# Reordering the head of a fused state-space and gated-MLP kernel: which engine copies tiles 0 and 1, when tile 2 and tile 3 are normalised, and where tile 2 and tile 3 are transposed

## The chip, the cores and the metric

The kernel runs on one core of a Trainium2 chip. The metric is the device time of one execution in microseconds (us), the median of several runs. A profile of one execution, taken by the hardware profiler, gives every instruction of the five engines: TensorE (PE, its weight loads are shown as PEld), VectorE (DVE), ScalarE (ACT), GpSimd (POOL) and SyncE (SP, which issues most DMAs).

## The reference

The input x has 2048 tokens of 448 features. Each row is normalised, xn = (x - mean) / sqrt(var + 1e-5). Two branches read xn:

```
Bu = xn @ B_bar^T ; h[t] = Lam_bar * h[t-1] + Bu[t] (complex, 448 states)
s  = 2 * Re(h @ C^T) + xn * Dskip
m  = (sigmoid(xn @ w_gate) * (xn @ w_up)) @ w_down     (448 -> 1792 -> 448)
out = x + s * silu(m)
```

## The kernel before, in words

The 2048 tokens are worked in four chunks of 512, each of four tiles of 128 tokens. TensorE contracts over partitions, so it needs xn with the features on the partitions: every tile is transposed. For chunks 1 to 3 a DMA does that. For chunk 0, at the head of the kernel, where everything waits for the first tiles, TensorE transposes each normalised tile against an identity matrix into PSUM and ScalarE or VectorE copies the result to SBUF (`xnT`).

The path of a tile of chunk 0 is: statistics (`bn` and `aggr` on VectorE, lines 431 to 439; for tile 2 `act_mean` and `act_var` on ScalarE, lines 471 to 477), square root on ScalarE (`root`, `act_root`, lines 466 and 479), reciprocal and normalisation on VectorE (`recip`, `norm`, lines 462 and 514), transposition on TensorE (`pe_transpose`, line 542, for tile 0; `row_transpose`, line 561, for tiles 1 to 3), and the copy (`pe_transpose` itself for tile 0, one half by VectorE and one by ScalarE; `pair_copy`, line 554, for tile 1; `row_copy`, line 572, for tiles 2 and 3: tile 2's halves go to ScalarE and VectorE, tile 3's both to VectorE).

The 448 features are held as 7 blocks of 64 rows. The products use half of the array's rows at a time: two products run side by side, one on the lower 64 rows (LO) and one on the upper 64 (UP), each 64 rows deep. A step of the gate product (one m of seven, 256 of the 1792 columns) has two PSUM banks, and each bank takes seven such products. `z_mm` (line 783) issues the pair with one product for each bank; `ph_mm(u, 0)` (line 791) issues three pairs in which LO writes bank 0 and UP bank 1; `ph_mm(u, 1)` issues three pairs the other way round. When a bank is to be written by the other half of the rows than before, `row_mm` makes the product wait until the other half's last product there is done:

```
774   pe_n[0] += 1
775   other = None if start else wrote.get((bank, 1 - h))
...
778   if other and other[0] > seen[0]:
779       tc.add_manual_dep(T.nop().ins, other[1].ins.name, SYNC, reason="other rows' product in this bank")
```

The nop's wait is put on the weight load or product behind it.

The first three gate steps of chunk 0 cannot wait for all four tiles, so they are cut (lines 1111 and 1112): `units[t]` holds tile t's 128 tokens of steps 0 and 1 (banks gu0 and gu1), `pairs[0]` and `pairs[1]` the tokens of tiles 0 and 1, and of 2 and 3, of step 2 (gu2, 256 tokens). `front` (line 1120) of a list issues `ph_mm(u, 0)` and `z_mm(u)` of each unit, `back` (line 1125) issues `ph_mm(u, 1)`. Before the change TensorE's order is: tile 0's transposition; `columns` (line 602), five small products that turn three parameter rows into columns, in the bank of tile 0's second half; `fill(5)`, five products that nothing uses; tile 1's transposition, into gu2; front and back of unit 0; front of unit 1; tile 2's transposition, into the two `acc` banks; back of unit 1; front of pair 0; front of unit 2; tile 3's transposition; back of unit 2; back of pair 0; front of unit 3; front of pair 1; back of unit 3; back of pair 1. Gate step 3 follows in the `acc` banks (`one(0, 3, "g", ...)`, line 1173), and then all other work of chunk 0. The results of steps 0 to 2 leave PSUM through ScalarE (`gu_evac`, line 843, Tanh at line 853).

The order on the engines comes from a planner inside the kernel (`Plan`). Each operation is added with an engine, a cost, the keys it reads and writes, and for the head (`pl.seq = True`) TensorE, VectorE and ScalarE keep the order in which operations are added. Behind the head (line 1172 on) VectorE and ScalarE choose by due times that the planner works out, so a change of the head can move their later operations. SyncE and the DMA issues keep their order. `gate` adds a point without an instruction, which orders keys. `silu_table` (line 636) loads the second activation table on ScalarE once all square roots are done, `turns` and `scale` start the rotation tables on GpSimd and ScalarE.

Of the kernel before, what the change touches and what calls it, by code (L numbers as in the profile page):

```python
# [14 lines left out]
ACT = mybir.ActivationFunctionType  # L15
# [6 lines left out]
P = 128  # L22
# [52 lines left out]
class Plan:  # L75
# [10 lines left out]
    def add(self, eng, cost, fn, r=(), w=(), dma=0, lat=None, chain=False, name="", rate=230e3):  # L86
        o = Op()
        o.idx, o.eng, o.cost, o.fn, o.dma, o.name = len(self.ops), eng, cost, fn, dma, name
        o.lat = LAT.get(eng, 0.0) if lat is None else lat
        o.pre, o.suc, o.rate = {}, [], rate  # L90
        o.slot, o.land = None, 0.0
        if dma and eng != "POOL":
            o.slot, self.n_dma = self.n_dma, self.n_dma + 1
        o.start = o.end = None
        for k in r:
            if k in self.w:
                self._edge(self.w[k], o, True)
        for k in w:
            for q in self.r.get(k, ()):
                self._edge(q, o, False)  # L100
            if k in self.w:
                self._edge(self.w[k], o, True)
        for k in w:
            self.w[k] = o
            self.r[k] = []
        for k in r:
            if k not in w:
                self.r.setdefault(k, []).append(o)
        if chain or eng == "PE" or (eng in ("DVE", "ACT") and self.seq):
            key = ("chain", eng)  # L110
            if key in self.last_of:
                self._edge(self.last_of[key], o, None)
            self.last_of[key] = o
        self.ops.append(o)
        return o
# [132 lines left out]
def kernel(  # L248
# [213 lines left out]
    def recip(t0, n):  # L462
        ks = lambda k: [(k, t) for t in range(t0, t0 + n)]
        add("DVE", 0.08, lambda: V.reciprocal(out=rsd[:, t0:t0 + n, :], in_=sdb[:, t0:t0 + n, :]), r=ks("sd"), w=ks("rs"))

    def root(t, n=1):
        ts = range(t, t + n)
        add("ACT", 0.2, lambda: A.activation(sdb[:, t:t + n, :], mvf[:, t:t + n, 1:2], ACT.Sqrt, bias=epsc[:]),
            r=[("mv", q) for q in ts] + ["sqrttab", "epsc"], w=[("sd", q) for q in ts], lat=0.16)
# [5 lines left out]
    def act_var(t):  # L475
        add("ACT", 0.7, lambda: A.activation(junk[:], x_all[:, t, :], ACT.Square, bias=nmf[:, t, :], accum_out=sqf[:, t, :]),
            r=[("x", t), ("nf", t)], w=[("mv", t), "junk"])
# [36 lines left out]
    def norm(t, eng="DVE"):  # L514
        b, o, x = xkey(t), pieces(xbuf(t), 256, 256), pieces(x_all[:, t, :], 192, 256)
        if t < TPC:
            s1, op0 = (nmf[:, 2, :], ALU.add) if t == 2 else (mvf[:, t, 0:1], ALU.subtract)
            e, cost = (V, 0.36) if eng == "DVE" else (G, 0.7)
            add(eng, cost, lambda: e.tensor_scalar(out=o, in0=x, scalar1=s1, scalar2=rsd[:, t, :], op0=op0, op1=ALU.mult),  # L519
                r=[("x", t), ("mv", t), ("rs", t)], w=[("xn", b)])  # L520
        else:
            r = [("x", t), ("rs", t), ("nm", t)]
            if t < 2 * TPC:
                add("DVE", 0.36, lambda: V.tensor_scalar(out=o, in0=x, scalar1=rsd[:, t, :], scalar2=nmr[:, t, :],
                                                         op0=ALU.mult, op1=ALU.add), r=r, w=[("xn", b)])
            else:
                add("ACT", 0.7, lambda: A.activation(o, x, ACT.Identity, bias=nmr[:, t, :], scale=rsd[:, t, :]), r=r, w=[("xn", b)])
# [14 lines left out]
    def pe_transpose(t, keys, banks):  # L542
        o, js = xbuf(t), slice(t * P, t * P + P)
        for i, (key, bank) in enumerate(zip(keys, banks)):
            tp = flat(bank.bitcast(BF16)[:, 0:2 * P], 2, P)

            def f(i=i, tp=tp):
                for s in range(2):
                    T.transpose(tp[:, s, :], o[:, (2 * i + s) * P:(2 * i + s + 1) * P], ident[:, :])  # L549
            add("PE", 0.15, f, r=[("xn", xkey(t)), "ident"], w=[key])  # L550
            eng, cost, e = (("DVE", 0.28, V.tensor_copy), ("ACT", 0.33, A.copy))[i]
            add(eng, cost, lambda e=e, i=i, tp=tp: e(out=xnT[0][:, 2 * i:2 * i + 2, js], in_=tp), r=[key], w=[("xnT", 0, t, i)])

    def pair_copy(t, a, eng):
        js = slice(t * P, t * P + P)
        src = gu[a][:].bitcast(BF16)[:, :, 0:4 * H].rearrange("p h (s j) -> p s h j", j=H)
        e, cost = (A.copy, 0.57) if eng == "ACT" else (V.tensor_copy, 0.45)
        add(eng, cost, lambda: e(out=xnT[0][:, :, js].rearrange("p s (h j) -> p s h j", j=H), in_=src),
            r=[("gu", a, 0), ("gu", a, 1)], w=[("xnT", 0, t, 0), ("xnT", 0, t, 1)])

    def row_transpose(t, keys, banks):
        o = xbuf(t)
        tp = [flat(bank.bitcast(BF16)[:, 0:4 * H], 4, H) for bank in banks]

        def f():
            for s in range(4):
                for h, (hs, _, _) in enumerate((LO, UP)):
                    T.transpose(tp[h][:, s, :], o[hs, s * P:s * P + P], ident[hs, hs])
        add("PE", 0.13, f, r=[("xn", xkey(t)), "ident"], w=keys)
        return tp  # L570

    def row_copy(t, h, key, tp):
        js = slice(t * P + h * H, t * P + h * H + H)
        eng, cost, e = (("ACT", 0.33, A.copy), ("DVE", 0.25, V.tensor_copy))[h or t == 3]
        add(eng, cost, lambda: e(out=xnT[0][:, :, js], in_=tp), r=[key], w=[("xnT", 0, t, h)])
# [60 lines left out]
    def silu_table():  # L636
        add("ACT", 1.3, lambda: A.preload_act_table_set("silu_and_others"), r=[("sd", t) for t in range(4)] + [("xnT", 0, 2, 0), "pv0"], w=["silutab"])
# [153 lines left out]
    def ph_mm(u, i, qs=(0, 1, 2), start=False, stop=False):  # L791
        out, w, x, r, keys, banks, n, name = u

        def f():
            for q in qs:
                for h, (hs, ss, _) in enumerate((LO, UP)):
                    b = 1 - h if i else h
                    row_mm(banks[b], h, lambda: T.matmul(out[b], lhsT=w(b, hs, ss[q]), rhs=x(b, hs, ss[q]),  # L798
                                                         start=start and q == 0, stop=stop and q == 2), start and q == 0)
        add("PE", len(qs) * (0.0028 + n / 2400.0), f, r=r, w=keys, name=name)  # L800
# [295 lines left out]
    u2 = slots0[2]  # L1096
# [6 lines left out]
    aggr(1)  # L1103
    norm(0)
    root(1)
    act_var(2)
    recip(1, 1)
    norm(1)
    uk, ub = [("gu", u2, 0), ("gu", u2, 1)], [gu[u2][:, 0, :], gu[u2][:, 1, :]]
    ak, ab = [("acc", 0), ("acc", 1)], [acc[0][:], acc[1][:]]  # L1110
    units = [[gu_unit(0, "g", m, slots0[m], t, t + 1) for m in range(2)] for t in range(TPC)]
    pairs = [gu_unit(0, "g", 2, u2, t, t + 2) for t in (0, 2)]

    def fill(n):
        def f():
            for _ in range(n):
                T.matmul(gu[slots0[0]][:, 0, 0:P], lhsT=ones[:, 0:P], rhs=ones[:, 0:P], start=True, stop=True)  # L1117
        add("PE", 0.055 * n, f, w=[("gu", slots0[0])])

    def front(us, start=False):  # L1120
        for u in us:
            ph_mm(u, 0, start=start)
            z_mm(u, False)

    def back(us, stop=False):
        for u in us:
            ph_mm(u, 1, stop=stop)

    pe_transpose(0, ak, ab)
    copy_pv = columns(acc[1][:, 400:412], "pvps")  # L1130
    fill(5)
    act_root(2)
    row_transpose(1, uk, ub)
    pair_copy(1, u2, "ACT")
    bn(3)
    recip(2, 1)
    norm(2)
    aggr(3)
    copy_pv()
    add("NONE", 0.0, lambda: None, r=["pv0", ("xn", 0)], w=["pv"], lat=0.0)  # L1140
    front(units[0], True)
    back(units[0])
    front(units[1])
    root(3)
    tp = row_transpose(2, ak, ab)
    for h in range(2):
        row_copy(2, h, ak[h], tp[h])
    recip(3, 1)
    norm(3)
    silu_table()  # L1150
    back(units[1])
    gate(uk, ("gu", u2))
    front(pairs[0:1], True)
    front(units[2])
    tp = row_transpose(3, ak, ab)
    for h in range(2):
        row_copy(3, h, ak[h], tp[h])
    back(units[2])
    back(pairs[0:1])
    turns()  # L1160
    scale(0)
    front(units[3])
    front(pairs[1:])
    back(units[3], True)
    back(pairs[1:], True)
    gu_evac(0, "g", 0, slots0[0])
    gu_evac(0, "g", 1, slots0[1])
    gu_evac(0, "g", 2, slots0[2])
# [113 lines left out]
```

## Time and profile before

| | us |
|---|---|
| median of 3 runs (lowest, highest) | 182.67 (182.58, 182.85) |
| the profiled execution's own time | 182.58 |
| its span, first to last instruction | 180.8 |
| around the span | 1.78 |
| DVE busy | 162.3 (90%) |
| ACT busy | 107.2 (59%) |
| POOL busy | 26.4 (15%) |
| tile 0's transposition starts on PE | 5.32 |
| gate step 3 starts on PE | 11.59 |

The span begins with the first instruction and ends with the last; the time has what lies around it as well. A matmul's row has its start and a modelled end; products are pipelined, so the next one starts before the row of the one before ends. A line of the timeline merges rows of one kind that follow each other: start, length, engine, line of the kernel, operation, what it writes and reads, shape and count. In brackets stands how long the engine was idle ahead of it and what ended that.

### The profile page before, as it was taken

The numbers are of one execution on the slowest core, as the hardware profiler recorded it, in microseconds if no ns is written. First come the engines' busy times: TensorE is split into PE (matmuls) and PEld (weight loads), VectorE is DVE, ScalarE is ACT, GpSimd is POOL, SyncE is SP. The second block draws the span as 40 slices with busy tenths as digits, with TensorE's granted clock in tenths as the row PEclk, the third lists the DMA queues.
The fourth block names the chain that finished last, engine by engine and source line by source line (L and its number), as shares of the span: only waits on it lengthen the run. The fifth ranks groups of instructions, "written<-read, shape, count | busy, mean of one in ns | idle before, by whom it ended". The sixth has DMA issues, their size and how long they took to land.

```text
span 180.8 us, 3804 instructions
## 1 busy us (share of the span) xinstructions
PE 176.8 (98%) x1507; PEld 89.5 (49%) x1507; DVE 162.3 (90%) x300; ACT 107.2 (59%) x175; POOL 26.4 (15%) x76
## 2 busy tenths in 40 slices
PE   8999999999999999999999999999999999999993
PEld 2775555564544444445554444454554444455552
DVE  2776899999997889999999998999999999999572
ACT  3889992966698898473265333599221599711100
POOL 5374224000028118600000000000000000000000
DMA  5999833998000320000032000000000000012131
GB/s 151 370 362 243 127 60 63 300 235 231 1 0 0 62 58 0 4 0 0 4 62 56 0 4 0 0 29 25 25 2 4 0 0 0 4 51 75 54 119 39
DMA packets 23941, 12.73 MB, mean 70 GB/s; under 512 B 14833, under 2 KB 23922, under 8 KB 23922
## 3 DMA queue, kind: packets, MB, share of 16 engines
q1 hardware_dynamic: 23568, 12.24, 26.9%
q8 instruction: 12, 0.20, 0.5%
q10 hardware_dynamic: 290, 0.23, 0.4%
q14 instruction: 7, 0.06, 0.1%
q0 software_dynamic: 64, 0.00, 0.0%
HBM read 7.23 MB, written 1.84 MB: 50 GB/s over the span
## 4 chain that ended last, share of the span: by engine, by line
PE 95%; DMA 2%; DVE 1%; SPq 0%; issue 0%; DVEq 0%
PE gu L798 42%; PE gu L1015 15%; PE acc L1034 10%; PE acc L1015 9%; PE acc L798 9%; PE gu L788 7%; DMA x_all<-in_A_x_dram 2%; PE gu L1034 1%; PE acc L788 1%; DVE o_t L1076 0%; DVE bst L433 0%; DVE o_t L1070 0%; PE acc L549 0%; SPq L360 0%; PE gu L1117 0%; DVE g_t L519 0%
## 5 line engine op out<-in xcount | busy, mean ns | idle before, releaser
L798 PE MATMUL gu<-xnT,wU 64*128 64x512 bf16 x288 | 41.8, 376 | 0.0
L798 PE MATMUL gu<-xnT,wG 64*128 64x512 bf16 (+2 forms) x348 | 37.9, 325 | 0.0
L1015 PEld LDWEIGHTS <-hF 128*128 128x128 bf16 x224 | 21.7, 98 | 21.2 <-issue 1.3
L1015 PE MATMUL gu<-wd,hF 128*128 128x448 bf16 x140 | 28.0, 352 | 0.0
L798 PEld LDWEIGHTS <-wG 64*128 64x128 bf16 x420 | 19.2, 94 | 17.2 <-issue 0.2
L798 PEld LDWEIGHTS <-wU 64*128 64x128 bf16 x336 | 17.0, 94 | 18.6 <-PE gu L798 0.2
L954 DVE TENSOR_TENSOR_SCAN wv<-c_r,st,z 128x512 bf16<-128x512 f32 x18 | 22.9, 1277 | 0.0
L1021 ACT ACTIVATE g_t<-gu 128x448 bf16<-128x448 f32 x10 | 5.4, 543 | 28.8 <-PE gu L1015 28.7
L853 ACT ACTIVATE sig<-gu 128x1024 f32<-128x1024 f32 x16 | 16.3, 1022 | 9.5 <-PE gu L798 9.3
L1034 PE MATMUL acc<-cT,hT 128*128 128x448 bf16 (+2 forms) x105 | 20.0, 335 | 0.0
L798 PE MATMUL gu<-xnT,bT 64*128 64x512 bf16 x144 | 19.3, 376 | 0.0
L861 DVE SCALAR_TENSOR_TENSOR hF<-sig,gu 128x1024 bf16<-128x1024 f32 x13 | 15.8, 1218 | 2.2 <-PE gu L798 2.0
L1015 PE MATMUL acc<-wd,hF 128*128 128x448 bf16 x84 | 16.9, 353 | 0.0
L1034 PEld LDWEIGHTS <-hT 128*128 128x128 bf16 x126 | 11.7, 98 | 9.9 <-issue 0.4
L904 ACT CAST bus<-gu 128x1024 bf16<-128x1024 f32 x12 | 11.9, 1013 | 6.9 <-PE gu L798 6.6
L798 PEld LDWEIGHTS <-bT 64*128 64x128 bf16 x192 | 9.7, 94 | 8.8 <-issue 1.1
L798 PE MATMUL acc<-xnT,wG 64*128 64x512 bf16 x72 | 10.6, 376 | 0.0
L910 ACT CAST bus<-acc 64x256 bf16<-64x256 f32 (+1 forms) x24 | 8.6, 369 | 2.7 <-PE acc L798 2.5
L788 PE MATMUL gu<-xnT,wG 64*128 64x512 bf16 (+2 forms) x58 | 9.6, 325 | 0.0
L853 ACT ACTIVATE sig<-acc 128x512 f32<-128x512 f32 x10 | 5.6, 592 | 6.6 <-PE acc L798 6.6
L433 DVE BATCH_NORM_STATS2 bst<-x_all 128x6 f32<-128x448 bf16 x11 | 6.5, 615 | 3.3 <-DMA x_all<-in_A_x_dram 3.3
L788 PE MATMUL gu<-xnT,wU 64*128 64x512 bf16 x48 | 9.2, 376 | 0.0
(161 smaller groups left out, 271.2 us busy)
## 6 DMA issues: line engine op xcount, KB each, us to landing
wd<-in_B_w_down_dram SPq DMA_DIRECT2D x2, 784.0 KB, 5.9
x_all<-in_A_x_dram SPq DMA_DIRECT2D x6, 224.0 KB, 4.1
wG<-in_B_w_gate_dram SPq DMA_DIRECT2D x4, 256.0 KB, 4.1
wU<-in_B_w_up_dram SPq DMA_DIRECT2D x4, 256.0 KB, 6.2
out_dram<-o_t SPq DMA_DIRECT2D x8, 112.0 KB, 1.7
wG<-in_B_w_gate_dram SPq DMA_DIRECT2D x2, 384.0 KB, 5.7
wU<-in_B_w_up_dram SPq DMA_DIRECT2D x2, 384.0 KB, 6.9
out_dram<-ctmp SPq DMA_DIRECT2D x6, 112.0 KB, 1.7
```

What stands on the lines that cost most here:

```text
L433: add("DVE", 0.56 if t < TPC else 0.6, lambda: V.bn_stats(out=bst[b][:], in_=x_all[:, t, :]), r=[("x", t)] + ([("xnT", 0, 3, 1)] if 3 < t ...
L788: row_mm(banks[b], b, lambda: T.matmul(out[b], lhsT=w(b, hs, s), rhs=x(b, hs, s), start=start, stop=False), start)
L798: row_mm(banks[b], h, lambda: T.matmul(out[b], lhsT=w(b, hs, ss[q]), rhs=x(b, hs, ss[q]), start=start and q == 0, stop=stop and q == 2), s ...
L853: add("ACT", act(n), lambda s=s, src=src: A.activation(th[:, s, :], src, ACT.Tanh, scale=0.5), r=keys, w=[tk])
L861: add("DVE", dve1(n), lambda s=s, src=src: V.scalar_tensor_tensor(out=ho[:, s, :], in0=th[:, s, :], scalar=1.0, in1=src, op0=ALU.add, op1= ...
L904: add("ACT", act(1024), lambda: A.copy(out=bus[u][:], in_=gu[slots[pt]][:]), r=key(pt), w=[("bus", u)])
L910: add("ACT", 0.36, lambda ns=ns, d=d, q=q, l=l, i=i: A.copy(out=bus[u][d, l, ns], in_=acc[a3[i]][q, 0:256]), r=[("acc", a3[i])] + ([("bus" ...
L954: dve(1.194, lambda k=k: V.tensor_tensor_scan(out=wv[:, k, :], data0=rb, data1=z[:, k, :], initial=(st[pt][:, k, :] if c else 0.0), op0=AL ...
L1015: T.matmul(d, lhsT=hF[c % 2][:, m, h, js], rhs=wd[:, ft, :], start=(ft == 0), stop=(ft == FT - 1))
L1021: add("ACT", act(448), lambda: A.activation(g_t[g][:], d, ACT.Silu, scale=0.5), r=[key, "silutab"], w=[("gt", g)])
L1034: T.matmul(y, lhsT=hT[c % 2][:, hm, js], rhs=cT[:, cm, c0:c1], start=(i == 0 and not skip_on_pe), stop=(i == 6))
```

## The change

Tile 0's second half is copied by ScalarE ahead of tile 2's variance (`act_var(2)` moves behind it). Tile 1's pair is copied by VectorE instead of ScalarE. Tile 3's statistics and square root stand ahead of tile 2's reciprocal and normalisation, and tile 3's reciprocal and normalisation follow directly. `fill(5)` becomes `fill(2)`. Unit 1's back follows its front directly; tile 2 is transposed inside pair 0, between `ph_mm(pairs[0], 0)` and `z_mm(pairs[0])`, and tile 3 behind pair 0's back. Tiles 2 and 3 are transposed into different columns of the `acc` banks, with keys of their own. Unit 2, unit 3 and pair 1 are then each issued as front and back without another unit between.

```diff
     norm(0)
     root(1)
-    act_var(2)
     recip(1, 1)
     norm(1)
     uk, ub = [("gu", u2, 0), ("gu", u2, 1)], [gu[u2][:, 0, :], gu[u2][:, 1, :]]
-    ak, ab = [("acc", 0), ("acc", 1)], [acc[0][:], acc[1][:]]
...
-    pe_transpose(0, ak, ab)
+    def to_acc(t):
+        c0 = (t - 2) * P
+        keys = [("tp", t, i) for i in range(2)]
+        return keys, row_transpose(t, keys, [a[:, c0:c0 + P] for a in acc])
+
+    pe_transpose(0, ["tp0", "tp1"], [a[:] for a in acc])
     copy_pv = columns(acc[1][:, 400:412], "pvps")
-    fill(5)
+    fill(2)
+    act_var(2)
     act_root(2)
     row_transpose(1, uk, ub)
-    pair_copy(1, u2, "ACT")
+    pair_copy(1, u2, "DVE")
     bn(3)
-    recip(2, 1)
-    norm(2)
     aggr(3)
     copy_pv()
     add("NONE", 0.0, lambda: None, r=["pv0", ("xn", 0)], w=["pv"], lat=0.0)
+    root(3)
+    recip(2, 1)
+    norm(2)
+    recip(3, 1)
+    norm(3)
     front(units[0], True)
     back(units[0])
     front(units[1])
-    root(3)
-    tp = row_transpose(2, ak, ab)
-    for h in range(2):
-        row_copy(2, h, ak[h], tp[h])
-    recip(3, 1)
-    norm(3)
-    silu_table()
     back(units[1])
     gate(uk, ("gu", u2))
-    front(pairs[0:1], True)
+    ph_mm(pairs[0], 0, start=True)
+    k2, tp2 = to_acc(2)
+    for h in range(2):
+        row_copy(2, h, k2[h], tp2[h])
+    z_mm(pairs[0], False)
+    back(pairs[0:1])
+    k3, tp3 = to_acc(3)
+    for h in range(2):
+        row_copy(3, h, k3[h], tp3[h])
+    silu_table()
     front(units[2])
-    tp = row_transpose(3, ak, ab)
-    for h in range(2):
-        row_copy(3, h, ak[h], tp[h])
     back(units[2])
-    back(pairs[0:1])
     turns()
     scale(0)
     front(units[3])
+    back(units[3], True)
     front(pairs[1:])
-    back(units[3], True)
     back(pairs[1:], True)
+    gate(["tp0", "tp1", "pvps", *k2, *k3], [("acc", 0), ("acc", 1)])
     gu_evac(0, "g", 0, slots0[0])
```

## The prediction

> **What bounds the kernel now.** I read the page first, then the list of TensorE's waits, then its timeline in the head. From the page: span, busy time, and the chain that ended last.
>
> ```profile
> span 180.8 us, 3804 instructions
> ...
> PE 176.8 (98%) x1507; PEld 89.5 (49%) x1507; DVE 162.3 (90%) x300; ACT 107.2 (59%) x175; POOL 26.4 (15%) x76
> ...
> PE 95%; DMA 2%; DVE 1%; SPq 0%; issue 0%; DVEq 0%
> ```
>
> TensorE carries 95% of the chain, and the list of its waits holds only 0.8 us at the very start. Yet a product's row lasts longer than the distance to the next product, so a short wait doesn't show as idle time; it shows in the starts. TensorE's timeline in the head:
>
> ```profile
> 5.95 0.46 PE L1117 MATMUL gu<-const-bfloat16-1.0 128*128 128x128 bf16 x5
> 6.34 0.29 PE L568 MATMUL gu<-ident,g_t 64*128 64x64 bf16 x8
> 6.47 0.33 PE L798 MATMUL gu<-xnT,wG 64*128 64x128 bf16 x6
> 6.64 0.22 PE L788 MATMUL gu<-xnT,wG 64*128 64x128 bf16 x2
> 6.69 0.33 PE L798 MATMUL gu<-xnT,wG 64*128 64x128 bf16 x6
> 6.86 0.22 PE L788 MATMUL gu<-xnT,wG 64*128 64x128 bf16 x2
> 6.92 0.75 PE L798 MATMUL gu<-xnT,wG 64*128 64x128 bf16 x18
> 7.51 0.22 PE L788 MATMUL gu<-xnT,wG 64*128 64x128 bf16 x2
> ...
> 10.82 0.29 PE L788 MATMUL gu<-xnT,wG 64*128 64x256 bf16 x2
> 10.93 0.84 PE L798 MATMUL gu<-xnT,wG 64*128 64x128 bf16 x18
> 11.59 0.40 PE L788 MATMUL acc<-xnT,wG 64*128 64x512 bf16 x2
> ```
>
> See three things. Unit 0's front is 8 pairs from 6.47 to 6.92: 0.056 us a pair. The next row has 9 pairs (unit 0's back, and 3 of unit 1's front) and takes 0.59 to 7.51, where 9 x 0.056 = 0.50: so 0.08 was waiting. At the end of the head pair 0's kind (256 wide) costs 0.107 a pair, and gate step 3 starts at 11.59. Where the waits are, the weight loads (PEld) show. One in a narrow window at 7.14, one in the timeline of the whole head:
>
> ```profile
> 7.14 0.10 PEld L798 LDWEIGHTS <-wG 64*128 64x128 bf16 x2
> ```
>
> ```profile
> 10.05 0.17 PEld L798 LDWEIGHTS <-wG 64*128 64x128 bf16 x5 [0.16 <-issue]
> ```
>
> The load at 7.14 is the second half of unit 0's back, on a bank that the other rows wrote last in the product of 6.86. That row ends at 6.86 + 0.22 = 7.08; the load follows 0.06 later. The load at 10.05 is unit 3, which waits for tile 3's copies on VectorE (9.50 to 9.99): 0.15 late. Behind 10.05 I found in TensorE's starts one more wait, 0.11 at 149.3, and nothing else: what the head loses or gains, the end loses or gains.
>
> **The change part by part.**
>
> *The start.* The part of the copy that is moved forward on ScalarE gains nothing by itself. From the timeline of all engines, 5.8 to 6.1:
>
> ```profile
> 5.76 0.19 ACT L476 ACTIVATION_READ_ACCUMULATOR junk<-x_all,nmf 128x1 f32 x1
> 5.83 0.19 PE L609 MATMUL acc<-ident,hF 3*64 3x3 bf16 x2
> ...
> 6.06 0.37 ACT L552 COPY xnT<-acc 128x256 bf16<-128x256 bf16 x1
> ```
>
> ScalarE was free at 5.95 (5.76 + 0.19), and copied at 6.06. The end before that is the last product of `columns`, 5.83 + 0.19 = 6.02, in the same bank: the program gives TensorE one signal for tile 0's second half and `columns` together, before and after the change. So the copy stays at 6.06 to 6.43, and `act_var(2)`, now behind it, moves from 5.20 to 6.33 (ScalarE's next instruction came 0.27 after the copy's start). Three fills fewer are 3 x 0.06 = 0.18, so tile 1's transposition starts at 6.16 and unit 0 at 6.29; but its fourth product needs ScalarE's half, 6.43 + 0.04 = 6.47, where it stood at 6.53 before. Gain: **0.06**, not 0.18. From the other side: a copy right behind tile 0's second half could start at 5.78, and the gain would be the full 0.18; I take 0.06, as the signal decides.
>
> *Tile 1 on VectorE.* ScalarE's row for this copy is 0.58 (L558). VectorE has no such row; half as many elements took 0.28 (L552), normalising 512 from SBUF 0.41 (L519). I take 0.42 (0.28, and 0.13 for the other half by the difference of these two), from 6.50 (transposition done at 6.46) to 6.92. The upper bound is by a VectorE row that reads fp32 from PSUM, 448 in 0.62 (L1056): 0.71 for 512. Unit 1 follows unit 0 at 7.27 (7.33 - 0.06), so the copy is covered even then (7.21). [...]
>
> *Tile 2 and tile 3.* ScalarE: variance 6.33 to 7.07 (0.74 with the accumulator's read), root to 7.40, `copy_pv` to 7.49. VectorE: tile 1's copy to 6.92 (next instruction at 6.83), `bn(3)` 6.83 to 7.45, `aggr` to 7.66, `recip(2)` at 7.58, `norm(2)` 7.78 to 8.19. Tile 2 can be transposed at 8.25. TensorE comes there later (below, 8.47), so this later chain is covered by 0.2. `norm(3)` ends at 8.72.
>
> *Waits between the two halves of the rows.* This is what the change adds. `front` and `back` of units 1, 2 and 3 now follow each other directly, as only unit 0's did: **3 x 0.08 = 0.24**. Before, a transposition (units 1 and 2) or pair 1's front (unit 3) stood between. And pairs 0 and 1 get `z_mm` directly ahead of `back`: each bank is then written by the other half of the rows with nothing between. The wait is the row's length 0.27 (256 wide, as the row of 8.56) plus the 0.06 seen at 7.14, in place of 0.107: 0.33 - 0.107 = 0.22, with the first weight load's 0.01 **0.23 each, 0.46**. Before, 12 or more other products stood there. [...]
>
> *The wait at 10.05 goes:* tile 3 is transposed at 9.25 and copied by about 10.12, unit 3 starts at 10.23: **gain 0.15**. Tile 3's transposition now shares a bank with tile 2's copies and waits for ScalarE's, which ends at 9.15 (8.78 + 0.37): covered by pair 0's wait (back until 9.25); without that wait it would stall TensorE by 0.17.
>
> The line of starts is then: unit 0's fourth product 6.47, unit 1 7.27, pair 0 8.14, tile 2 8.47, `z_mm` 8.58, back 8.92, tile 3 9.25, unit 2 9.37, unit 3 10.23, pair 1 11.09, its back 11.75, gate step 3 12.09. Steps of it: a unit with its back directly behind its front 0.86 (unit 0: 6.47 to 7.33); three 256 wide pairs 0.33 (8.24 to 8.57); a transposition 0.12 (7.79 to 7.90); `z_mm` and its wait 0.11 + 0.23.
>
> *Covered.* GpSimd's `turns` start 0.15 later (`copy_pv` 7.49 for 7.34); ScalarE's table load moves from 8.49 to 9.17 and `scale(0)` to 10.47, its end 11.08 for the next instruction, beside which bank gu0 is done at 11.03; it must be free at 12.95 (12.45 + 0.5), and Tanh takes 1.02. If that cover went, TensorE would wait the rest. Pair 0's last weight block lands at 8.08, just ahead of its use at 8.15. SyncE's order is unchanged. Behind the head the planner orders some of VectorE's and ScalarE's work anew; each PSUM bank has about three steps of 1.5 us to be emptied, so I cost it at nothing; bounds -0.11 (the wait at 149.3 gone) and +1.2 (one L861, 1.22, in front of an awaited one), nearer to zero, since only one such wait exists now.
>
> **Sum:** -0.06 + 0.24 + 0.46 - 0.15 = 0.49, the line of starts gives 12.09 - 11.59 = 0.50. Against the profiled execution 182.58 + 0.5 = 183.08 (span 181.3 and 1.78 around); that execution is the lowest of three, 0.09 under the median, so the median to expect is **183.17**.
>
> **The rivals.**
> - *The pairs' waits are hidden.* The trace has no direct `z_mm` to `back` at 256. If it goes at the usual 0.107, tile 3 stalls on ScalarE's copy instead (0.17 of 0.23 stays) and only pair 1's 0.23 is saved with 0.06: 182.88. [...] Against it: 7.14.
> - *Not slower: no row wait reaches the path at all.* Place: all five joints. Then unit 1 starts at 7.17, pair 0 at 7.95, tile 2 at 8.33, and tile 3 waits for tile 2's copy by ScalarE (8.33 + 0.31 + 0.37, and 0.04) until 9.06; unit 2 at 9.17, unit 3 at 9.98, pair 1 at 10.76, step 3 at 11.52: 0.07 earlier, 182.60. It decides only if the five joints together cost under 0.1 instead of 0.70. Against it: 0.08 measured at unit 0.
> - *VectorE or a bank becomes the bound.* The copy at 0.71 makes tile 2 late by 0.07 (8.25 + 0.29 against 8.47); a reordered evacuation adds one wait like that at 10.05 (0.15) up to 1.2: 183.25 to 184.4. For it: VectorE is 90% busy. Against: no wait of this kind now.
> - *The change doesn't do what it says* (ScalarE's copy no earlier) is in my forecast.
>
> **How the numbers follow.** Forecast 0.62, pairs hidden 0.12, not slower 0.08, a new bound 0.18. The likeliest case's own range is 183.0 to 183.35. The range 182.75 to 183.6 leaves out the not-slower case and the upper half of the last. A measurement of this kernel tells apart about 0.2%, 0.37 us. Slower by more (over 183.04): most of the forecast and the last, 0.75; within: 0.22; faster by more (under 182.30): 0.03, as the gains in sight are 0.06 + 0.15 + 0.11.
>
> **What would show it.** In the profile after: ScalarE's L552 copy still at 6.06; weight loads 0.33 behind the 256 wide `z_mm` twice; no idle PEld for unit 3; step 3's first product at about 12.1. It is wrong if step 3 starts before 11.7, or if it starts at 12.1 and the end doesn't follow.

## The result, and the profile after

| | before | after |
|---|---|---|
| median, us (lowest to highest, 16 runs each) | 182.75 (182.45 to 183.06) | 183.12 (182.94 to 184.87) |
| ratio after to before, 95% interval | | 1.0027, 1.0016 to 1.0037 |
| profiled execution, its own time | 182.58 | 183.22 |
| its span | 180.8 | 181.5 |
| tile 0's transposition starts | 5.32 | 4.90 |
| `columns` starts | 5.67 | 5.84 |
| unit 0's fourth product | 6.53 | 6.64 |
| gate step 3 starts | 11.59 | 12.25 |

The change makes the kernel slower by 0.27%, 0.49 us (0.29 to 0.68 by the interval; the medians lie 0.37 apart). The page of the changed kernel, the lines that answer to those of before:

```profile
span 181.5 us, 3795 instructions
...
PE 176.7 (97%) x1504; PEld 87.1 (48%) x1504; DVE 163.2 (90%) x301; ACT 106.4 (59%) x174; POOL 26.4 (15%) x76
...
PE 95%; DVE 1%; DMA 1%; issue 1%; SPq 0%; DVEq 0%
```

TensorE still carries 95% of the chain, with three products fewer (1504 for 1507) and 176.7 us busy for 176.8. Nothing on this page says where 0.6 us of span came from. The head's timeline does. First its start:

```profile
5.84 0.21 PE L607 MATMUL acc<-ident,hF 3*128 3x3 bf16 x3 [0.54 <-issue]
...
5.98 0.19 PE L609 MATMUL acc<-ident,hF 3*64 3x3 bf16 x2
...
6.21 0.37 ACT L552 COPY xnT<-acc 128x256 bf16<-128x256 bf16 x1 [1.33 <-PE acc L609]
...
6.45 0.46 PE L798 MATMUL gu<-xnT,wG 64*128 64x128 bf16 x6
...
6.66 0.42 DVE L558 COPY xnT<-gu 128x512 bf16<-128x512 bf16 x1 [0.93 <-PE gu L568]
```

ScalarE's copy of tile 0 (L552) now stands ahead of tile 2's variance in ScalarE's order. ScalarE was idle for 1.33 us before it, and what ended that is the last product of `columns` (L609), not tile 0's transposition (4.90 to 5.30). The copy starts 0.23 behind that product's start, 6.21 - 5.98, as before (6.06 - 5.83). Unit 0's six products from 6.45 take 0.46 in place of 0.33: the fourth waits for this copy. Then the two pairs, each in its own stretch of the timeline:

```profile
8.62 0.28 PE L568 MATMUL acc<-ident,g_t 64*128 64x64 bf16 x8
...
8.73 0.27 PE L788 MATMUL gu<-xnT,wG 64*128 64x256 bf16 x2
...
9.07 0.22 PEld L798 LDWEIGHTS <-wG 64*128 64x128 bf16 x6 [0.26 <-PE gu L788]
...
9.41 0.28 PE L568 MATMUL acc<-ident,g_t 64*128 64x64 bf16 x8
```

```profile
11.57 0.27 PE L788 MATMUL gu<-xnT,wG 64*128 64x256 bf16 x2
...
11.91 0.22 PEld L798 LDWEIGHTS <-wG 64*128 64x128 bf16 x6 [0.34 <-PE gu L788]
...
12.25 0.38 PE L788 MATMUL acc<-xnT,wG 64*128 64x512 bf16 x2
```

Both times the weight load behind `z_mm` comes 0.334 after it and the product 0.338, where products of this width otherwise follow each other at 0.109: 0.229 of waiting, by the starts of the single rows. The bracket names what ended it: `z_mm`'s own product. This is the wait that `row_mm` puts into the program. No run leaves it out, so what the products would do without it is not shown.

Two distances are used from here on, both from the starts of single rows in the trace. **The head** is the way from unit 0's fourth product to step 3's first: 5.06 us before, 5.61 after. **The rest**, from step 3 to the last instruction, is 169.22 before and 169.20 after. So the loss lies in the head, and the 0.11 by which the fourth product itself came later lies ahead of it: `columns` started 0.17 later in this execution, and the way from `columns` to the fourth product became 0.06 shorter.

### The profile page after: what moved, and what is told of

Its sections match the earlier page's. It is cut to its first block, busy times and chain, and to the rows that moved or that the text cites. A ratio compares the mean times of both kernels' runs of the same rounds, so it can differ in the third digit from the quotient of the medians.

```text
span 181.5 us, 3795 instructions
## 1 busy us (share of the span) xinstructions
PE 176.7 (97%) x1504; PEld 87.1 (48%) x1504; DVE 163.2 (90%) x301; ACT 106.4 (59%) x174; POOL 26.4 (15%) x76
## 4 chain that ended last, share of the span: by engine, by line
PE 95%; DVE 1%; DMA 1%; issue 1%; SPq 0%; DVEq 0%
PE gu L798 42%; PE gu L1015 15%; PE acc L1034 10%; PE acc L1015 9%; PE acc L798 9%; PE gu L788 7%; PE gu L1034 1%; PE acc L788 1%; DMA x_all<-in_A_x_dram 1%; DVE o_t L1076 0%; DVE bst L433 0%; DVE o_t L1070 0%; PE acc L549 0%; SPq L360 0%; DVE g_t L519 0%
## 5 line engine op out<-in xcount | busy, mean ns | idle before, releaser
L798 PEld LDWEIGHTS <-wG 64*128 64x128 bf16 x420 | 18.3, 94 | 18.4 <-PE gu L788 0.6
L798 PEld LDWEIGHTS <-wU 64*128 64x128 bf16 x336 | 16.3, 94 | 19.2 <-PE gu L798 0.2
L798 PEld LDWEIGHTS <-bT 64*128 64x128 bf16 x192 | 9.1, 94 | 9.4 <-issue 1.1
```

## The experiments

The theory: TensorE's order decides. A half row product that writes a bank right behind the other half's product is made by `row_mm` to wait for that row to end (a joint, from here on), and the change puts five such joints in place of one wait for copies. The rival: the joints are hidden or free, and the loss comes from the start, a late tile, or the engines behind the head.

| kernel | `columns` to fourth product | head | rest | median | ratio to before, 95% |
|---|---|---|---|---|---|
| before | 0.86 | 5.06 | 169.22 | 182.75 | |
| changed | 0.79 | 5.61 | 169.20 | 183.12 | 1.0016 to 1.0037 |
| e1: before, pair 1 joined | 0.85 | 5.38 | 169.22 | 182.96 | 1.0002 to 1.0020 |
| e2: changed, old end | 1.00 | 5.45 | 169.20 | 183.00 | 1.0001 to 1.0018 |
| e3: changed, three switches | 0.82 | 6.10 | 169.21 | 183.65 | 1.0035 to 1.0059 |
| e4: changed, own signal | 0.87 | 5.63 | 169.21 | 183.37 | 1.0016 to 1.0055 |
| e7: the same again | 0.67 | 5.64 | 169.20 | 183.15 | 1.0021 to 1.0047 |
| e8: changed again | 0.79 | 5.62 | 169.21 | 183.12 | 1.0020 to 1.0038 |
| e5: before, no wait | 0.85 | 4.92 | 169.25 | 182.73 | 0.9997 to 1.0020 |
| e6: no wait, own signal, two fills | 1.25 | 4.92 | 169.20 | 182.41 | 0.9973 to 0.9992 |
| e12: no wait, two fills | 0.83 | 4.92 | 169.21 | 182.54 | 0.9982 to 1.0006 |
| e9: before, two fills | 0.80 | 5.05 | 169.24 | 182.81 | 0.9993 to 1.0012 |
| e10: before, engine moves alone | 0.80 | 5.56 | 169.23 | 183.11 | 1.0012 to 1.0030 |
| e11: changed, joints apart | 0.79 | 5.37 | 169.20 | 183.00 | 1.0000 to 1.0028 |

The first three columns are from each kernel's one profile; before stood at 182.74 to 182.77 beside the experiments. The rest is the same in all fourteen traces within 0.06 us: in the profiled executions these edits act ahead of step 3 alone.

**One joint put into the kernel before (e1).**

```diff
     front(units[3])
+    back(units[3], True)
     front(pairs[1:])
-    back(units[3], True)
     back(pairs[1:], True)
```

> The kernel before with one thing of the change: pair 1's front moved behind unit 3's back, so that pair 1's back follows its own z_mm directly, and unit 3's back its own front. Theory (half-row products of one bank wait for each other): the weight load behind pair 1's z_mm comes 0.33 us after it instead of 0.107, and unit 3's joint costs 0.05 to 0.08: +0.28 to +0.31 us against the kernel before, and gate step 3 that much later measured from unit 0's first product (5.12 before). Rival (joints are free, the change's loss lies in the start or behind the head): step 3 at the same distance, time within 0.1 us of before.

Its timeline where pair 1 ends:

```profile
11.26 0.27 PE L788 MATMUL gu<-xnT,wG 64*128 64x256 bf16 x2
...
11.59 0.22 PEld L798 LDWEIGHTS <-wG 64*128 64x128 bf16 x6 [0.34 <-PE gu L788]
...
11.93 0.38 PE L788 MATMUL acc<-xnT,wG 64*128 64x512 bf16 x2
```

The 0.34 of the changed kernel's pair 1, made by this one move. From unit 0's first product to step 3 it is 5.44 for 5.12, +0.32; the median rose by 0.19, and the interval (0.04 to 0.37 us) holds 0.3. The time alone is too coarse for the rival's "within 0.1"; the head, 0.32 longer, leaves it out.

**The same joint taken out of the changed kernel (e2).**

```diff
     front(units[3])
-    back(units[3], True)
     front(pairs[1:])
+    back(units[3], True)
     back(pairs[1:], True)
```

> The changed kernel with the old order at the head's end: pair 1's front stands between unit 3's front and back again. Theory: the 0.23 us behind pair 1's z_mm and unit 3's 0.05 go: step 3's first product 0.28 us nearer to unit 0's fourth product (5.33 instead of 5.615), and the time 0.28 us under the changed kernel, about 0.2 above the kernel before. Rival (joints are free): the same distance, the time of the changed kernel.

```profile
11.31 0.27 PE L788 MATMUL gu<-xnT,wG 64*128 64x256 bf16 x2
...
11.42 0.82 PE L798 MATMUL gu<-xnT,wG 64*128 64x128 bf16 x18
...
12.09 0.38 PE L788 MATMUL acc<-xnT,wG 64*128 64x512 bf16 x2
```

The next product follows 0.11 behind `z_mm`; the 0.23 is gone, and unit 3's 0.05 too. The head shrank by 0.16, not by 0.28: in this execution pair 0's last weight block landed late and held its products at 8.54 by 0.09 (the row waits on a DMA's semaphore), and the products of unit 0 behind the fourth went at half pace, some 0.05 (last section). So the joint's size is as expected in the rows. The median lies 0.12 under the changed kernel's, with intervals that overlap, and is too coarse to show it.

**More switches, the same products (e3).**

```diff
-    front(pairs[1:])
-    back(pairs[1:], True)
+    p1 = pairs[1]
+    ph_mm(p1, 0, (0,))
+    ph_mm(p1, 1, (0,))
+    ph_mm(p1, 0, (1, 2))
+    z_mm(p1, False)
+    ph_mm(p1, 1, (1, 2), stop=True)
```

> The changed kernel with pair 1's 14 products in another order: one pair of products to one bank each, one pair crossed, three pairs straight, two crossed. So the halves of the rows change banks three times in place of once, with the same products. Theory: each change costs 0.23 us, so +0.46 us against the changed kernel, about +0.95 against the kernel before; step 3 6.07 us behind unit 0's fourth product in place of 5.615. Rival (the order of the products doesn't matter, only how many there are): no change against the changed kernel.

The weight loads in its timeline where pair 1 is worked:

```profile
11.52 0.10 PEld L798 LDWEIGHTS <-wG 64*128 64x128 bf16 x2 [0.29 <-PE gu L798]
...
11.87 0.12 PEld L798 LDWEIGHTS <-wG 64*128 64x128 bf16 x4 [0.25 <-PE gu L798]
...
12.43 0.11 PEld L798 LDWEIGHTS <-wG 64*128 64x128 bf16 x4 [0.34 <-PE gu L788]
```

Three waits where one was: 0.23, 0.24 and 0.23 by the single rows. The head became 0.49 longer than the changed kernel's (0.46 expected), the median 0.53. No product was added, so this is the price of the order alone, and it grows with the number of switches.

**Tile 0's second half with a signal of its own (e4, and again as e7 beside the changed kernel, e8).**

```diff
-    copy_pv = columns(acc[1][:, 400:412], "pvps")
+    copy_pv = columns(gu[u2][:, 0, 400:412], "pvps")
...
-    gate(uk, ("gu", u2))
+    gate([*uk, "pvps"], ("gu", u2))
...
-    gate(["tp0", "tp1", "pvps", *k2, *k3], [("acc", 0), ("acc", 1)])
+    gate(["tp0", "tp1", *k2, *k3], [("acc", 0), ("acc", 1)])
```

> The changed kernel with the parameter columns written to the bank of tile 1's transposition instead of the bank of tile 0's second half. TensorE now gives a signal right behind tile 0's second half, which ScalarE's copy waits for. Theory (ScalarE's copy was held by the columns' products, not by ScalarE's order): the copy starts 0.06 to 0.1 us behind tile 0's last transposition row, ahead of the columns' end, and unit 0's fourth product no longer waits (0.13 us of extra distance in the changed kernel): 0.13 to 0.18 us faster than the changed kernel, about 0.35 above the kernel before. Rival (the copy is late for another reason, or unit 0 waits for something else): L552 on ScalarE still about 0.37 us behind the columns' first product, and the time of the changed kernel.

> The changed kernel with the parameter columns in the bank of tile 1's transposition, once more, beside the changed kernel itself on the same chip: its first runs scattered from 182.82 to 185.06 us, while its trace had lost the 0.13 us at unit 0's fourth product. Theory (scatter of the early transfers): 0.1 to 0.15 us under the changed kernel here. Rival (the bank shared with tile 1's copy makes the kernel slower in executions that the profile didn't catch): 0.2 us over the changed kernel again.

> The changed kernel itself, as the partner for the other runs of this call. Theory: 0.35 to 0.5 us over the kernel before; in its trace the same waits as in the first profile (0.23 behind z_mm of pairs 0 and 1, 0.05 in each unit, none for tile 3's copies) and the distance from unit 0's fourth product to step 3 5.615 us again, however the early transfers land. Rival (the head's start differs from run to run by the kernel's own doing): another distance.

The timeline of e7 at the start:

```profile
5.48 0.37 ACT L552 COPY xnT<-acc 128x256 bf16<-128x256 bf16 x1 [0.61 <-PE acc L549]
...
5.69 0.21 PE L607 MATMUL gu<-ident,hF 3*128 3x3 bf16 x3 [0.25 <-issue]
```

Now tile 0's transposition (L549) releases the copy, and it runs ahead of `columns`: the claim about the signal is shown. In e7 the fourth product stood 0.67 behind `columns`, for 0.79 in the changed kernel: the 0.13 is gone from the trace. The medians show no gain: 183.37 and 183.15 against 183.12, but their intervals (e7's is from five runs) are wide enough to hide 0.13. The trace of e4 shows one way in which it can be given back (TensorE's first rows went at half pace there, the two fills 0.39 long for the changed kernel's 0.29, and the fourth product stood at 0.87). Whether that is what the timed runs met, no profile shows; this stays open. The bank shared with tile 1's copy makes no wait in either trace. The changed kernel's second profile repeated its head to 0.002 us (5.616 for 5.614), with `columns` 0.25 earlier.

**Neither wait nor joint (e5).** The kernel before, in another order:

```diff
     bn(3)
+    aggr(3)
     recip(2, 1)
     norm(2)
-    aggr(3)
+    root(3)
+    recip(3, 1)
+    norm(3)
     copy_pv()
...
     front(units[1])
-    root(3)
     tp = row_transpose(2, ak, ab)
     for h in range(2):
         row_copy(2, h, ak[h], tp[h])
-    recip(3, 1)
-    norm(3)
...
     front(pairs[0:1], True)
-    front(units[2])
     tp = row_transpose(3, ak, ab)
     for h in range(2):
         row_copy(3, h, ak[h], tp[h])
+    front(units[2])
+    ph_mm(pairs[0], 1, (0,))
     back(units[2])
-    back(pairs[0:1])
+    ph_mm(pairs[0], 1, (1, 2))
```

> The kernel before, rearranged so that neither the wait for tile 3's copies nor any of the change's joints is left: tile 3's statistics and norm ahead of VectorE's copy of tile 2, tile 3 turned right behind pair 0's z_mm, and pair 0's back cut in two, one pair of products between unit 2's front and back, two behind unit 2's back. Theory (the head's distance is the products plus the waits at joints and for copies): the 0.149 us at unit 3 goes and nothing comes for it, so step 3 stands 4.91 us behind unit 0's fourth product in place of 5.06, and the time is 0.15 us under the kernel before. Rival (the wait at unit 3 was hidden, or tile 2 or a bank is late in its place): 5.06 or more, no gain.

Unit 3's first weight loads in its timeline have no idle time ahead of them:

```profile
9.77 0.26 PEld L798 LDWEIGHTS <-wG 64*128 64x128 bf16 x6
```

The head is 4.92 in place of 5.06, 0.144 shorter, and unit 0's 0.05 is the only wait left in it. The time did not follow: 182.73 for 182.74, and the interval (0.05 under to 0.37 over before) leaves out the 0.15. The profiled execution, 182.59, is one of the shorter ones; four of the twelve runs stand over 183.0, where one of 29 of the kernel before does. Why is not known, since no profile caught such a run.

**The same with the start's two edits (e6), and with the fills alone (e12).** e6 adds e4's lines to e5 and puts `fill(2)` for `fill(5)`; e12 has only the fills.

> The kernel before rearranged as in the run without the wait at unit 3, and besides the parameter columns in the bank of tile 1's transposition (a signal of tile 0's own for ScalarE's copy), with two fills in place of five. Theory: ScalarE's copy starts when its variance is done, about 0.1 us earlier than in the kernel before, unit 0 starts 0.1 to 0.17 us nearer to the columns' products, tile 1's copy on ScalarE then costs up to 0.06: 0.05 to 0.1 us faster than the run without these two edits, 0.2 to 0.25 us under the kernel before. Rival (a faster start is given back to the weight block that pair 0 waits for): no gain against that run, and a wait of pair 0's products on a DMA queue's signal.

> The kernel before rearranged as in the run without the wait at unit 3, with two fills in place of five, and the parameter columns where they were. It parts the two edits by which the fastest run so far differs from the one without the wait. Theory (steps add up): unit 0's fourth product 0.79 us behind the columns' first product, step 3 4.92 us behind the fourth product, so 0.144 + 0.06 = 0.20 us under the kernel before. If the time is 0.33 us under, as that fastest run was, the signal of tile 0's own is worth nothing beside the fills; if it is about the kernel before's, that signal is worth the whole 0.3.

Both have e5's head, 4.92. In e12's profile the fourth product stood at 0.83 instead of the 0.79 expected, with TensorE's rows at half pace until about 6.5. e6 is 0.33 under the kernel before (0.15 to 0.49 by the interval), the only kernel here that is surely faster than both; e12 is 0.22 under by the median, with an interval that holds zero. In e6's profile the start was bound by something else again:

```profile
6.80 0.28 PE L798 MATMUL gu<-xnT,wG 64*128 64x128 bf16 x3 [0.35 <-DMA wG<-in_B_w_gate_dram]
```

The fourth product waited for the second weight block, which landed at 6.75 in this execution, and at 5.99 to 6.59 in the others. That profile's own time, 182.69, is the highest of e6's runs. So the traces put the rearranged head at 0.14, and its worth in time stays unsettled: the medians of e5, e12 and e6 lie 0.01, 0.22 and 0.33 under the kernel before. What the single edits of the start add is not to be had from them either: e12's and e6's fall below e5's by 0.19 and 0.32, where their steps give 0.06 and about 0.1.

**Two fills alone (e9).**

```diff
-    fill(5)
+    fill(2)
```

> The kernel before with two fills in place of five and nothing else. Theory (ScalarE's half of tile 0, held by the columns' signal, decides unit 0's fourth product): TensorE's first product of unit 0 comes 0.18 us nearer to the columns, but its fourth product only 0.06 us: 0.79 us behind the columns' first product in place of 0.856; time 0.06 us under the kernel before, too little to be told from none. Rival (the fills decide): 0.68 us and 0.18 us faster.

0.80 for 0.86: 0.06 won of 0.18, and the time the same. Unit 0's first product came 0.19 nearer, and the fourth then waited 0.13 for ScalarE.

**The engine moves without TensorE's new order (e10).** The kernel before with the change's edits ahead of `front(units[0], True)` only:

```diff
     root(1)
-    act_var(2)
...
-    fill(5)
+    fill(2)
+    act_var(2)
...
-    pair_copy(1, u2, "ACT")
+    pair_copy(1, u2, "DVE")
     bn(3)
-    recip(2, 1)
-    norm(2)
     aggr(3)
...
+    root(3)
+    recip(2, 1)
+    norm(2)
+    recip(3, 1)
+    norm(3)
     front(units[0], True)
...
-    root(3)
...
-    recip(3, 1)
-    norm(3)
```

> The changed kernel's order on ScalarE and VectorE and its two fills, with TensorE's order of the kernel before (tile 2 turned inside unit 1, units and pairs interleaved, no direct joint but unit 0's). Theory: tile 2's norm ends at about 8.3 instead of 7.27 us, so TensorE waits for it inside unit 1, where it came at 7.79 before: 0.5 to 0.6 us; of this 0.06 is won at the start, and the wait for tile 3's copies stays about 0.1: +0.45 to +0.55 us against the kernel before. Rival (the late norm of tile 2 is covered in either order): the time of the kernel before.

TensorE and its weight loads where tile 2 is transposed:

```profile
8.48 0.17 PEld L568 LDWEIGHTS <-g_t 64*128 64x128 bf16 x8 [0.51 <-DVE g_t L519]
8.48 0.29 PE L568 MATMUL acc<-ident,g_t 64*128 64x64 bf16 x8 [0.34 <-DVE g_t L519]
```

A wait of 0.50 for tile 2's norm on VectorE. This is what the changed kernel's order covers, and the head is 5.56, nearly the changed kernel's 5.61. The median is 0.35 over the kernel before (0.22 to 0.55 by the interval), where 0.45 to 0.55 was expected. The change thus makes tile 2 late, hides that by moving its transposition behind unit 1, and pays for the hiding in joints about what it would have paid in waiting: 183.12, and 183.11 here.

**The joints apart (e11).** e2's edit, and

```diff
     ph_mm(pairs[0], 0, start=True)
+    z_mm(pairs[0], False)
     k2, tp2 = to_acc(2)
     for h in range(2):
         row_copy(2, h, k2[h], tp2[h])
-    z_mm(pairs[0], False)
     back(pairs[0:1])
```

> The changed kernel with the old order at the head's end (pair 1's front between unit 3's front and back), and tile 2's transposition between pair 0's z_mm and back instead of ahead of z_mm. Theory: pair 1's 0.23 and unit 3's 0.05 go, of pair 0's 0.23 the transposition hides 0.11; but tile 3's transposition, which waits for ScalarE's copy of tile 2, is then late by 0.15 to 0.2: step 3 stands 5.39 us behind unit 0's fourth product in place of 5.615, the time 0.22 us under the changed kernel. Rival (tile 3's transposition doesn't wait for that copy): 5.22 us, 0.39 under the changed kernel.

```profile
8.69 0.37 ACT L575 COPY xnT<-acc 128x256 bf16<-128x256 bf16 x1 [0.87 <-PE acc L568]
...
9.11 0.29 PE L568 MATMUL acc<-ident,g_t 64*128 64x64 bf16 x8
```

Tile 3's transposition starts 0.05 behind the end of ScalarE's copy of tile 2 (8.69 + 0.37 = 9.06); by the single rows it is 0.173 late. Pair 0's joint fell to 0.11. Head 5.37 for 5.39 expected, not the rival's 5.22. The runs scatter from 182.62 to 183.98; their median, 0.12 under the changed kernel's, is too coarse for the 0.22 expected.

## Why the prediction was right, point by point

- **The sum.** Step 3 was to stand 0.50 later, the median at 183.17. Measured: head +0.55, start -0.06, so +0.49; the medians differ by 0.37, the ratio gives 0.49 (0.29 to 0.68). That 183.12 lies so near to 183.17 is partly luck: the forecast stood on a median of three runs, 182.67, which is 182.75 by sixteen, and the medians' rise was 0.13 less than forecast; the two partly cancel. The line of starts holds step by step: from unit 0's fourth product to tile 2, `z_mm`, pair 0's back, tile 3, unit 2, pair 1's back and step 3 it forecast 2.00, 2.11, 2.45, 2.78, 2.90, 5.28 and 5.62; the trace has 1.98, 2.10, 2.44, 2.77, 2.89, 5.28 and 5.61.
- **The pairs' joints, 0.23 each.** Measured 0.229 and 0.229, made in the kernel before by one move (e1), removed (e2), tripled (e3). What it is made of fits too: `row_mm`'s wait lasts until `z_mm`'s own product ends, and in the changed kernel the weight load comes 0.334 behind the start of that row, which is 0.27 long, so 0.06 behind its end as forecast. Where no such wait stands between two products of this width, the next one follows at 0.109 in the trace, for the 0.107 that the forecast took.
- **The units' joints, 0.08 each.** 0.045 at the second step's back, and some 0.04 more in the rows around it: from unit 0's back to unit 1's back (7.02, 7.89), and from unit 2's to unit 3's (9.98, 10.85), it is 0.87 us for 14 pairs, which at 0.056 take 0.78.
- **The wait at 10.05 goes, 0.15.** It is gone (0.149). Tile 3's wait for ScalarE's copy was covered by pair 0's joint as said; uncovered (e11) it is 0.173 for the 0.17 forecast.
- **The start, 0.06 and not 0.18.** 0.06, in the change and with the fills alone (e9); e7 shows that the signal was the reason. But the copy did not stay at 6.06: it came at 6.21, since `columns` waited for a parameter row. The distance was right and the moment was not.
- **VectorE's copy, 0.42.** Measured 0.42 (the row of 6.66, L558). The upper bound of 0.71, an estimate from the fp32 row of L1056, is out.
- **Covered.** Tile 2's later norm was covered in the change and costs 0.504 where it is not (e10). GpSimd's `turns` began 0.30 later instead of 0.15 (7.79 for 7.50), `scale(0)` at 10.61 instead of 10.47, with no effect: the rest stayed at 169.20.
- **The rivals.** No joint is hidden, so the first two fall. No engine or bank became a bound: behind step 3 the largest wait is again one of about 0.11, at 149.9 where it stood at 149.3.
- **What the prediction lacked.** It took the start of the head as fixed. The profiled execution came at 183.22 instead of 183.08; `columns` came 0.17 later in it, a matter of that execution. The same scatter may be why differences of 0.1 to 0.2 in the traces (e4, e5, e12) don't show surely in the medians; for the timed runs this is not shown.

## What to carry to other kernels

An order on TensorE is part of the cost, not only the list of its products: when two halves of the rows take turns on one PSUM bank and the program makes each wait for the other, put other work between the turns, or pay the wait. In e11 a transposition of 0.12 us between them took 0.12 off the 0.23; with unit 3's back between, six pairs of products at pair 1 in e2, nothing was left of it. An edit that covers a late input by moving work has to be charged with what that work stood between. Take distances between fixed events of the trace, here the fourth product and step 3: in the changed kernel's two profiles the head repeats to 0.002 us, in those of e4 and e7 to 0.014, where the times of whole runs scatter by 0.6. Then look whether the time follows: in e5 it didn't.

## What the runs showed of the hardware that was not expected

**TensorE's first rows run at half pace, and the moment at which that ends differs from execution to execution.** The same instructions in the changed kernel and in e2, from TensorE's timeline of each; first the changed kernel:

```profile
4.90 0.40 PE L549 MATMUL acc<-ident,g_t 128*128 128x128 bf16 x4 [0.19 <-DVE g_t L519]
...
6.10 0.29 PE L1115 MATMUL gu<-const-bfloat16-1.0 128*128 128x128 bf16 x2
6.32 0.29 PE L568 MATMUL gu<-ident,g_t 64*128 64x64 bf16 x8
```

and e2:

```profile
5.04 0.60 PE L549 MATMUL acc<-ident,g_t 128*128 128x128 bf16 x4
...
5.92 0.39 PE L1115 MATMUL gu<-const-bfloat16-1.0 128*128 128x128 bf16 x2
6.25 0.40 PE L568 MATMUL gu<-ident,g_t 64*128 64x64 bf16 x8
```

In the changed kernel the pace doubled at about 4.1 us (the warm-up rows of 512 columns go from 0.427 apart to 0.220), in e2 only at about 6.6, within unit 0; the granted clock of these stretches reads 1.00 in both. Counted from the start of the span the two moments lie 2.5 us apart, so the kernel's start alone does not fix them; what does is not shown. The highest times of the changed kernel and of e4, 184.87 and 185.06, stand 1.75 and 1.69 over their medians. No profile caught such a run, so whether a longer stretch at half pace made them is not shown either.

**Two transfers set the head's start.** `columns` began 0.09 behind the landing of the last parameter row in eleven of the fourteen profiles, with landings from 5.39 to 5.85, and 0.11 to 0.16 behind it in the other three; the second weight block landed at 5.99 to 6.75 and held unit 0's fourth product in two of them (e2 and e6). Issuing these earlier was not tried.
